# Staging the spatial weights earlier, and taking the high copies of normalized v from another source, in a fused attention and gated-MLP kernel

## The chip, the cores and the metric

The kernel runs as one program on one core of a Trainium2 chip. The metric is the time of one execution on the device in microseconds (us). Each version is timed in several runs, and one more execution is recorded by the hardware profiler. Every time below is of the kernel before the change.

## The reference

Three blocks follow each other on 4 batches of 576 tokens, 8 heads of 64, so 512 channels.

```python
# 1. attention, two masks: heads 0-3 local (the last 32 keys), heads 4-7 strided (every 32nd key)
scores = where(mask, q @ k.T / 8, -1e9)
attn   = exp(scores - max) / (sum + 1e-9)
x      = attn @ v                                    # [4, 576, 512]
# 2. gated block: v is normalized per token, then mixed over tokens
h = relu(x @ w_in);  u, v = h[..., :512], h[..., 512:]
v_n = (v - mean(v)) / sqrt(var(v) + 1e-6)            # over the 512 channels
v_s = einsum('ts,bsd->btd', w_spatial, v_n) + b_spatial
x   = (u * v_s) @ w_out
# 3. rotation block
theta = x @ w_theta
y = einsum(w_tok_r, x * cos(theta)) + einsum(w_tok_i, x * sin(theta))
u = x + y;  out = u + relu(u @ w_ch)
```

Inputs are float32. Square weights arrive as 64-bit words (float64 patterns viewed as integers), the spatial weights as float32.

## The kernel before

**Precision.** Large products run in float16 with a split: each operand is kept as a high part and a residual ("low"), and three passes (high by high, low by high, high by low) are added up in PSUM. So every operand costs a copy (high, mostly ScalarE) and a subtraction (low, VectorE or GpSimd) before it can be used.

**Tiling.** 576 tokens are four blocks of 128 and a tail of 64. Tiles of x, u and the rest lie transposed, channels on partitions; v lies with tokens on partitions, since it is normalized over channels. Blocks 0 and 1 of v make pair 0, blocks 2 and 3 pair 1. PSUM has three pairs of banks (tag "pm") that scores, v, u and all later products share, and two single banks ("sc", "av") for the attention of the following batches.

**The first attention** (`attention0`, line 658) has no other work to hide behind. It goes through nine groups of blocks in a pipeline of steps `s`: scores of group s, its exponentials, transposes of group s-1, the product with v of group s-2, and for group s-3 the transposed output, copied to `xT[0]` as high and low part (`gr_out`, line 617, ScalarE and then VectorE). Keys and queries of the two strided head pairs lie in the tile `xT[1]`, which is needed otherwise only when the attention of batch 1 writes its output there. Steps 9, 10 and 11 (`NG`, `NG+1`, `NG+2`) only drain the pipeline. In this phase every instruction keeps its place as written (`pinned`), on every engine and on the DMA-issuing queue SP.

Between the steps stand pieces of other work, given as a table (lines 1298 to 1309): the input weights `w_in` in four pieces of 1 MB, each with a load (`l0` to `l3`) and four conversion parts: two ScalarE passes in place on the 64-bit words (`a`, `b`), a VectorE combination (`c`), and the split (`e`: ScalarE high, GpSimd low). Pieces 0 and 1 are the v half, pieces 2 and 3 the u half. `go` emits the next stretch of the v product of batch 0; its last stretch reads channel block 3 of `xT[0]`, which the last groups of the attention write. `step` advances the attention of batch 1 (`attention1`, line 822): the first call loads, the second loads more and emits scores, softmax and division of its first step.

**After `pinned.clear()`** a planner orders the instructions of each engine by priorities and its own estimate of times. What is emitted when goes by a clock that counts the columns of the products emitted so far: `others()` (line 1272) takes a list `conv` of conversions with due times and the steps of the next attention. Instructions issued through `hv`, `ha`, `hg` stand 200 places ahead in priority.

**The spatial weights** (`sp_part`, line 306) are such conversions: two parts of 256 rows, loaded into the two raw staging buffers that the input weights used before (`stage()` alternates between `x2f` and `zf`), then a ScalarE copy with a scale and a VectorE residual into `wsp`. A tail of 64 rows and the bias follow (`sp_tail`).

**Normalizing v** (`norm`, `norm_q`, lines 1004 to 1027): statistics give mean and variance, `rstd` makes the reciprocal deviation by iterations on small tiles, VectorE normalizes each block in place in `vr`, ScalarE copies a pair to the high part of `vn`, VectorE subtracts for the low part. The spatial product of the first chunk reads both.

In the trace a load on SP waits, besides for its buffer, until the load eight places ahead of it in the queue has landed: the fourth piece for the third, the first load of spatial weights for the fourth piece.

Of the kernel before, what the change touches and what calls it, by code (L numbers as in the profile page):

```python
# [14 lines left out]
F32 = mybir.dt.float32  # L15
# [3 lines left out]
AF = mybir.ActivationFunctionType  # L19
ALU = mybir.AluOpType  # L20
# [25 lines left out]
E_VHI = 'aa'  # L46
# [12 lines left out]
CONV_SP = (20.0, 9.9, 1.9)  # L59
# [10 lines left out]
def kernel(  # L70
# [52 lines left out]
    nc = Engines  # L123
# [17 lines left out]
    B, DM, S = out.shape  # L141
    P = 128
    NC = DM // P
    NF = S // P
# [21 lines left out]
    hv, ha, hg = Ahead(nc.vector, AHEAD), Ahead(nc.scalar, AHEAD), Ahead(nc.gpsimd, AHEAD)  # L166
    H = {"v": hv, "a": ha, "g": hg}
    N = {"v": nc.vector, "a": nc.scalar, "g": nc.gpsimd}

    def copy(eng, key, dst, src):  # L170
        e = eng[key]
        if key == "a":
            e.activation(dst, src, AF.Copy)
        else:
            e.tensor_copy(dst, src)
# [30 lines left out]
    xT = [const.tile([P, 2, NC, S], F16, name=f"xT{i}") for i in range(2)]  # L206
    vn = const.tile([P, NF + 1, 2, DM], F16, name="vn")
# [9 lines left out]
    def s2(name):  # L217
        return scr.tile([P, 2, HS * 2], F32, tag="s2", name=name, bufs=4)
# [4 lines left out]
    def pm(name):  # L223
        return ps_m.tile([P, 2, 512], F32, tag="pm", name=name)
# [22 lines left out]
    def stage(late_raw=None):  # L247
        i = early[1]
        early[1] += 1
        if early[0]:  # L250
            return (raw0, raw1)[i % 2], vals[i % 2]
        return late_raw, s2("wx").rearrange("p a n -> p (a n)")
# [21 lines left out]
    def pair(ap, n):  # L274
        return ap[:, 0:2 * n].rearrange("p (a n) -> p a n", a=2)
# [12 lines left out]
    def prep_w(dst, src, c, i, late):  # L288
        for f in steps_w(dst, src, c, i, late):
            f()  # L290
# [11 lines left out]
    def sq_parts(dst, src, late=1):  # L302
        for i in range(0, NC, 2):
            yield lambda i=i: prep_w(dst, src, slice(0, DM), i, late)

    def sp_part(i):
        stg = pair(stage()[0].bitcast(F32), S)
        nc.sync.dma_start(stg, w_spT[i * P:(i + 2) * P, :].rearrange("(a p) n -> p a n", p=P))
        nc.scalar.activation(wsp[:, 0, i:i + 2, :], stg, AF.Copy, scale=SPS)
        nc.vector.scalar_tensor_tensor(wsp[:, 1, i:i + 2, :], stg, SPS, wsp[:, 0, i:i + 2, :],  # L310
                                       op0=ALU.mult, op1=ALU.subtract)
# [144 lines left out]
    NG = len(groups)  # L456
# [501 lines left out]
    def rstd(st, var, c):  # L958


        h, y, t = st[:, 0, c], st[:, 1, c], st[:, 2, c]
        hv.tensor_scalar(h, var, 1e-6, 0.5 / VNS ** 2, op0=ALU.add, op1=ALU.mult)
        hv.tensor_scalar(t.bitcast(I32), h.bitcast(I32), 1, None, op0=ALU.logical_shift_right)
        hv.tensor_scalar(y.bitcast(I32), t.bitcast(I32), -1, 0x5EF759DF - 2 ** 31, op0=ALU.mult, op1=ALU.add)
        for it in range(3):
            hv.tensor_tensor(t, y, y, ALU.mult)
            hv.tensor_tensor(t, t, h, ALU.mult)
            hv.scalar_tensor_tensor(y, t, 1.5, y, op0=ALU.subtract, op1=ALU.mult)

    def tail_mm(ps, x, w, cols):  # L970


        for n, (xe, we) in enumerate(PASS):
            for i in range(2):
                for h in range(2):
                    c = 2 * h + i
                    mm(ps[TL * h:TL * h + TL, :], x[:, xe, c, T0:S], w[:, we, c, cols],
                       start=(n == 0 and i == 0), stop=(n == 2 and i == 1))
                clock[0] -= DM

    def fold_tail(dst, tmp, ps):
        ha.activation(tmp, ps[TL:P, :], AF.Copy)
        hv.tensor_tensor(dst, ps[0:TL, :], tmp, ALU.add)

    def main_v(b):
        xh = xT[b % 2]
        vr = {}
        mv = mvs[:, b % 2]
        rs = att_p.tile([P, 3, 8], F32, tag="rs", name="rs")
        def v_relu(pr, ps):  # L990
            v = vr[pr] = s2(f"vr{pr}")
            if pr == 2:
                fold_tail(v[0:TL, 0, 0:DM], v[0:TL, 1, 0:DM], ps[:, 0, :])
                ha.activation(v[0:TL, 0, 0:DM], v[0:TL, 0, 0:DM], AF.Relu, scale=1.0 / PS)
                rows, nt = TL, 1
            else:
                ha.activation(v[:, :, 0:DM], ps, AF.Relu, scale=1.0 / PS)
                rows, nt = P, 2
            bs = att_p.tile([P, 2, 6], F32, tag="bs", name="bs")
            for t in range(nt):  # L1000
                hv.bn_stats(bs[0:rows, t, :], v[0:rows, t, 0:DM])
                hv.bn_aggr(mv[0:rows, 2 * pr + t, :], bs[0:rows, t, :])

        def norm(qs):
            c = slice(2 * qs[0], min(2 * qs[-1] + 2, 5))
            rstd(rs, mv[:, c, 1], c)
            for q in qs:
                norm_q(q)

        def norm_q(q):  # L1010
            rows = P if q < 2 else TL
            nt = 2 if q < 2 else 1
            for t in range(nt):
                i = 2 * q + t
                vv = vr[q][0:rows, t, 0:DM]
                hv.tensor_scalar(vv, vv, mv[0:rows, i, 0:1], rs[0:rows, 1, i:i + 1],
                                        op0=ALU.subtract, op1=ALU.mult)
            if q < 2:
                sv = vr[q][:, 0:2, 0:DM]
                copy(H, E_VHI[b > 0], vn[:, 2 * q:2 * q + 2, 0, :], sv)  # L1020
                H[E_VLO[q + 2 * (b > 0)]].tensor_tensor(vn[:, 2 * q:2 * q + 2, 1, :], sv,
                                                              vn[:, 2 * q:2 * q + 2, 0, :], ALU.subtract)
            else:
                sv = vr[2][0:TL, 0, 0:DM]
                copy(H, E_VHI[b > 0], vn[0:TL, 4, 0, :], sv)
                hv.tensor_tensor(vn[TL:P, 4, 0, :], sv, vn[0:TL, 4, 0, :], ALU.subtract)
                hg.tensor_copy(k2[0:TL], vn[0:TL, 4, 0, :])

        def v_mm(ps, i, c):
            for n, (xe, we) in enumerate(PASS):  # L1030
                clock[0] += DM
                marks.append((clock[0] / 2400.0, nc.tensor.matmul(
                    ps, xh[:, xe, c, i * P:(i + 1) * P], win[:, we, c, DM:2 * DM],
                    start=(c == 0 and n == 0), stop=(c == NC - 1 and n == 2)).ins.name))

        if b == 0:
            ps = [pm("v0")]

            def some(pr, cs, ts=(0, 1)):
                for t in ts:  # L1040
                    for c in cs:
                        v_mm(ps[pr][:, t, :], 2 * pr + t, c)

            for t in range(2):
                some(0, (0, 1), (t,))
                yield
            some(0, (2,))
            ps.append(pm("v1"))
            some(1, (0, 1))
            yield  # L1050
            some(1, (2,))
            yield
            for pr in range(2):
                some(pr, (3,))
                yield
                v_relu(pr, ps[pr])
            norm((0, 1))
        for pr in V_ORDER if b else V_ORDER[2:]:
            ps = pm(f"v{pr}")
            if pr == 2:  # L1060
                tail_mm(ps[:, 0, :], xh, win, slice(DM, 2 * DM))
                yield
            else:
                for t in range(2):
                    for c in range(NC):
                        v_mm(ps[:, t, :], 2 * pr + t, c)
                    yield
            v_relu(pr, ps)
        norm((2,) if b == 0 else (0, 1, 2))

    def main_mid(b):
# [164 lines left out]
    def timed(parts, due, lead, gap):  # L1236
        parts = list(parts)
        for i, f in enumerate(parts):
            conv.append((due - lead - gap * (len(parts) - 1 - i), f))

    timed([lambda i=i: sp_part(i) for i in range(0, NF, 2)] + [sp_tail], *CONV_SP)
    timed(sq_parts(wout, w_out), *CONV_OUT)
    timed(sq_parts(wth, w_th), *CONV_TH)
    conv.append((conv[-1][0], switch))
# [10 lines left out]
    for at, f in [(at, lambda n=n: tok_load(*toks[n])) for n, at in enumerate(TOK_AT)] + [  # L1255
            (at, lambda: next(atts[N32])) for at in PREP_AT]:
        i = next((i for i, c in enumerate(conv) if c[0] > at), len(conv))
# [32 lines left out]
    l1, a1, b1, c1, e1 = win_steps(1, 2)  # L1290
    l2, a2, b2, c2, e2 = win_steps(0, 0)
    l3, a3, b3, c3, e3 = win_steps(0, 2)
    v0 = main_v(0)

    def go():
# [6 lines left out]
        5: ((), (e0, l2)),  # L1302
        6: ((), (a1, b1)),
        7: ((), (c1, step)),
        8: ((), (e1, l3, go)),
        NG: ((), (go, step)),
        NG + 1: ((), (go, a2, b2, c2)),
        NG + 2: ((), (go, e2, a3, b3, c3, e3)),
    })
    pinned.clear()  # L1310
    run_main(v0)
# [93 lines left out]
```

## Time and profile before

| | us |
|---|---|
| median of 3 runs (lowest, highest) | 489.07 (488.37, 489.84) |
| profiled execution, whole | 488.06 |
| its span in the trace | 486.3 |
| TensorE matmul busy | 468.4 (96%) |
| VectorE busy | 300.8 (62%) |
| ScalarE busy | 267.2 (55%) |
| GpSimd busy | 71.4 (15%) |

Shares are means over stages with different limits: what a part of the program costs is read from the stage that it lies in. The granted clock of TensorE is 1.0 of full speed in all of the span. In the rows below, a timeline row gives the start, the length, the engine, the line (107 for all of them, since one helper issues every instruction), the operation, output and inputs, the tile's shape, how many were merged, and in brackets how long the engine had stood idle and what ended that.

### The profile page before, as it was taken

The numbers are of one execution on the slowest core, as the hardware profiler recorded it, in microseconds if no ns is written. First come the engines' busy times: TensorE is split into PE (matmuls) and PEld (weight loads), VectorE is DVE, ScalarE is ACT, GpSimd is POOL, SyncE is SP. The second block draws the span as 40 slices with busy tenths as digits, with TensorE's granted clock in tenths as the row PEclk, the third lists the DMA queues.
The fourth block names the chain that finished last, engine by engine and source line by source line (L and its number), as shares of the span: only waits on it lengthen the run. The fifth ranks groups of instructions, "written<-read, shape, count | busy, mean of one in ns | idle before, by whom it ended". The sixth has DMA issues, their size and how long they took to land. (4 is left out here: it accounts for less than half of the span.)

```text
span 486.3 us, 10776 instructions
## 1 busy us (share of the span) xinstructions
PE 468.4 (96%) x4440; PEld 352.3 (72%) x4440; DVE 300.8 (62%) x642; ACT 267.2 (55%) x470; POOL 71.4 (15%) x68
## 2 busy tenths in 40 slices
PE   7889889899999999999999999999999999999996
PEld 5665667676577778777568777777567777777775
DVE  3766998966998546752787878762686121227412
ACT  2657788879954334445945667754942022149202
POOL 2041124120015100201005100111005200210320
PEclk9999999999999999999999999999999999999999
DMA  6887666638760245100381345320450020003502
GB/s 179 288 243 208 201 224 217 195 154 245 161 148 1 69 163 148 54 0 1 86 217 52 91 123 158 67 44 1 74 122 1 2 98 0 1 2 76 121 0 99
DMA packets 71820, 52.72 MB, mean 108 GB/s; under 512 B 50584, under 2 KB 59992, under 8 KB 71770
## 3 DMA queue, kind: packets, MB, share of 16 engines
q1 hardware_dynamic: 71466, 51.42, 38.3%
q8 instruction: 35, 0.57, 0.5%
q10 hardware_dynamic: 304, 0.61, 0.4%
q14 instruction: 15, 0.12, 0.1%
HBM read 35.36 MB, written 4.72 MB: 82 GB/s over the span
## 5 line engine op out<-in xcount | busy, mean ns | idle before, releaser
L107 PE MATMUL y<-wtok,zf 128*128 128x288 f16 x864 | 107.2, 286 | 0.0
L107 PEld LDWEIGHTS <-zf 128*128 128x128 f16 x864 | 84.1, 98 | 22.2 <-issue 1.2
L107 PE MATMUL sp<-wsp,vn 128*128 128x288 f16 x384 | 50.3, 286 | 0.8 <-ACT u L107 0.8
L107 PE MATMUL x<-zf,wout 128*128 128x288 f16 x384 | 49.6, 287 | 0.0
L107 PE MATMUL u<-xT,win 128*128 128x288 f16 x384 | 49.3, 286 | 0.0
L107 PE MATMUL v<-win,xT 128*128 128x512 f16 (+1 forms) x240 | 48.4, 380 | 0.8 <-DVE xT L107 0.6
L107 PEld LDWEIGHTS <-vn 128*128 128x128 f16 x416 | 40.3, 98 | 11.2 <-issue 0.9
L107 PE MATMUL th<-x2h,wth 128*128 128x288 f16 x384 | 47.9, 286 | 0.3 <-DVE ta L107 0.3
L107 POOL TENSOR_TENSOR x2h<-x2f,x2h 128x576 f16<-128x576 f32 x19 | 26.6, 1403 | 142.7 <-issue 66.7
L107 PE MATMUL c<-x2h,wch 128*128 128x288 f16 x360 | 45.2, 286 | 0.0
L107 PEld LDWEIGHTS <-wth 128*128 128x128 f16 x384 | 37.6, 98 | 10.0 <-issue 0.5
L107 PEld LDWEIGHTS <-wch 128*128 128x128 f16 x384 | 37.4, 98 | 9.3
L107 PEld LDWEIGHTS <-win 128*128 128x128 f16 x384 | 37.4, 98 | 9.2
L107 PEld LDWEIGHTS <-wout 128*128 128x128 f16 x384 | 36.7, 98 | 9.5
L107 PEld LDWEIGHTS <-xT 128*128 128x128 f16 (+1 forms) x240 | 21.0, 100 | 25.3 <-issue 2.2
L107 ACT ACTIVATE x2h<-x2f 128x576 f16<-128x576 f32 (+1 forms) x28 | 20.9, 748 | 24.0 <-DVE x2f L107 23.5
L107 ACT ACTIVATE o<-c 128x576 f32<-128x576 f32 x15 | 9.7, 645 | 34.9 <-PE c L107 34.7
L107 DVE TENSOR_TENSOR ta<-ta,x2f 128x1152 f32<-128x1152 f32 (+1 forms) x17 | 21.7, 1284 | 11.2 <-ACT ta L107 11.2
L107 DVE SCALAR_TENSOR_TENSOR x2f<-y,x2f 128x576 f32<-128x576 f32 x16 | 12.1, 754 | 25.1 <-PE y L107 25.0
L107 DVE SCALAR_TENSOR_TENSOR o<-x2f,o 128x576 f32<-128x576 f32 (+1 forms) x17 | 12.2, 722 | 23.6 <-ACT o L107 23.6
L107 POOL TENSOR_TENSOR zf<-u,zf 128x576 f16<-128x576 f32 x8 | 10.2, 1277 | 112.9 <-ACT zf L107 112.9
L107 DVE TENSOR_TENSOR u<-u,sp 128x576 f32<-128x576 f32 x16 | 12.0, 750 | 22.4 <-PE sp L107 22.4
(146 smaller groups left out, 723.7 us busy)
## 6 DMA issues: line engine op xcount, KB each, us to landing
out_dram<-o SPq DMA_DIRECT2D x15, 288.0 KB
kt<-in_qp_dram SPq DMA_DIRECT2D x8, 288.0 KB
qs<-in_qd_dram SPq DMA_DIRECT2D x8, 288.0 KB
x2f<-in_w_in_dram SPq DMA_DIRECT2D x2, 1024.0 KB
zf<-in_w_in_dram SPq DMA_DIRECT2D x2, 1024.0 KB
xT<-in_w_ch_dram SPq DMA_DIRECT2D x2, 1024.0 KB
kt<-in_kzl_dram SPq DMA_DIRECT2D x8, 152.0 KB
ks<-in_kl_dram SPq DMA_DIRECT2D x4, 304.0 KB
```

What stands on the lines that cost most here:

```text
L107: ins = f(*args, **kwargs)
```

## The change

The two parts of the spatial weights no longer use the alternating staging buffers. They are loaded into `xT[1]` (`sp_place`, `sp_load`), issued behind the last load of input weights, and converted in step 11 of the first attention, no longer by the clock; only `sp_tail` stays in the timed list. In the table of the first attention the conversion of pieces 2 and 3 moves one step ahead (`a2`, `b2`, `c2` to step 9, `e2`, `a3`, `b3` to step 10), and the second `step` of batch 1 moves from step 9 to step 11, between the two conversions.

For batch 0, the high copies of the normalized v of the four full blocks are made by ScalarE from the unnormalized v with a per-partition scale (the reciprocal deviation) and bias (minus mean times that, one small VectorE product), one instruction for each block. VectorE's normalized v goes to other tiles (`vq` for pair 0, `vr[0]` for pair 1) and serves the residuals.

```diff
--- before.py
+++ after.py
@@ -303,9 +303,16 @@
         for i in range(0, NC, 2):
             yield lambda i=i: prep_w(dst, src, slice(0, DM), i, late)
 
+    raw_sp = xT[1].rearrange("p e c n -> p (e c n)").bitcast(F32)
+
+    def sp_place(i):
+        return raw_sp[:, i * S:(i + 2) * S].rearrange("p (a n) -> p a n", a=2)
+
+    def sp_load(i):
+        nc.sync.dma_start(sp_place(i), w_spT[i * P:(i + 2) * P, :].rearrange("(a p) n -> p a n", p=P))
+
     def sp_part(i):
-        stg = pair(stage()[0].bitcast(F32), S)
-        nc.sync.dma_start(stg, w_spT[i * P:(i + 2) * P, :].rearrange("(a p) n -> p a n", p=P))
+        stg = sp_place(i)
         nc.scalar.activation(wsp[:, 0, i:i + 2, :], stg, AF.Copy, scale=SPS)
         nc.vector.scalar_tensor_tensor(wsp[:, 1, i:i + 2, :], stg, SPS, wsp[:, 0, i:i + 2, :],
                                        op0=ALU.mult, op1=ALU.subtract)
@@ -1004,8 +1011,18 @@
         def norm(qs):
             c = slice(2 * qs[0], min(2 * qs[-1] + 2, 5))
             rstd(rs, mv[:, c, 1], c)
+            if b == 0 and qs[0] == 0:
+                hv.scalar_tensor_tensor(rs[:, 0, c], mv[:, c, 0], -1.0, rs[:, 1, c], op0=ALU.mult, op1=ALU.mult)
+                vr.update({3: s2("vq"), 4: vr[0]})
+                for i in range(4):
+                    ha.activation(vn[:, i, 0, :], vr[i // 2][:, i % 2, 0:DM], AF.Identity,
+                                  bias=rs[:, 0, i:i + 1], scale=rs[:, 1, i:i + 1])
             for q in qs:
                 norm_q(q)
+
+        def normed(q):
+
+            return q + 3 if b == 0 and q < 2 else q
 
         def norm_q(q):
             rows = P if q < 2 else TL
@@ -1013,11 +1030,12 @@
             for t in range(nt):
                 i = 2 * q + t
                 vv = vr[q][0:rows, t, 0:DM]
-                hv.tensor_scalar(vv, vv, mv[0:rows, i, 0:1], rs[0:rows, 1, i:i + 1],
+                hv.tensor_scalar(vr[normed(q)][0:rows, t, 0:DM], vv, mv[0:rows, i, 0:1], rs[0:rows, 1, i:i + 1],
                                         op0=ALU.subtract, op1=ALU.mult)
             if q < 2:
-                sv = vr[q][:, 0:2, 0:DM]
-                copy(H, E_VHI[b > 0], vn[:, 2 * q:2 * q + 2, 0, :], sv)
+                sv = vr[normed(q)][:, 0:2, 0:DM]
+                if b:
+                    copy(H, E_VHI[1], vn[:, 2 * q:2 * q + 2, 0, :], sv)
                 H[E_VLO[q + 2 * (b > 0)]].tensor_tensor(vn[:, 2 * q:2 * q + 2, 1, :], sv,
                                                               vn[:, 2 * q:2 * q + 2, 0, :], ALU.subtract)
             else:
@@ -1238,7 +1256,7 @@
         for i, f in enumerate(parts):
             conv.append((due - lead - gap * (len(parts) - 1 - i), f))
 
-    timed([lambda i=i: sp_part(i) for i in range(0, NF, 2)] + [sp_tail], *CONV_SP)
+    timed([sp_tail], *CONV_SP)
     timed(sq_parts(wout, w_out), *CONV_OUT)
     timed(sq_parts(wth, w_th), *CONV_TH)
     conv.append((conv[-1][0], switch))
@@ -1302,10 +1320,10 @@
         5: ((), (e0, l2)),
         6: ((), (a1, b1)),
         7: ((), (c1, step)),
-        8: ((), (e1, l3, go)),
-        NG: ((), (go, step)),
-        NG + 1: ((), (go, a2, b2, c2)),
-        NG + 2: ((), (go, e2, a3, b3, c3, e3)),
+        8: ((), (e1, l3, lambda: sp_load(0), lambda: sp_load(2), go)),
+        NG: ((), (go, a2, b2, c2)),
+        NG + 1: ((), (go, e2, a3, b3)),
+        NG + 2: ((), (go, c3, lambda: sp_part(0), e3, step, lambda: sp_part(2))),
     })
     pinned.clear()
     run_main(v0)
```

## Rows read from the trace of the kernel before

**Rows 1.** The page, busy us (share of the span) and instructions of each engine.

```profile
PE 468.4 (96%) x4440; PEld 352.3 (72%) x4440; DVE 300.8 (62%) x642; ACT 267.2 (55%) x470; POOL 71.4 (15%) x68
```

**Rows 2.** Stages: length, busy us of each engine, TensorE clock, DMA share, GB/s.

```profile
31.30:49.00 17.70, 17.38 (x156) 9.62 (x156) 10.51 (x26) 11.47 (x17) 6.41 (x7) 1.00 0.87 228
49.00:75.00 26.00, 22.85 (x236) 16.73 (x234) 25.88 (x70) 21.80 (x33) 7.33 (x7) 1.00 0.63 211
75.00:110.00 35.00, 32.05 (x419) 24.72 (x420) 28.16 (x49) 28.79 (x43) 7.56 (x6) 1.00 0.56 184
110.00:480.00 370.00, 367.96 (x3272) 279.56 (x3271) 214.87 (x442) 187.87 (x350) 44.67 (x31) 1.00 0.31 78
```

**Rows 3.** Timeline of TensorE.

```profile
36.01 0.73 PE L107 MATMUL a<-kt 64*64 64x96 f32 x16
...
37.95 4.06 PE L107 MATMUL v<-win,xT 128*128 128x512 f16 x18
...
42.07 5.46 PE L107 MATMUL v<-win,xT 128*128 128x512 f16 x30
...
58.49 0.61 PE L107 MATMUL av<-ident,sm 128*96 128x128 f32 x4 [1.52 <-ACT wspt L107]
...
62.34 1.63 PE L107 MATMUL sp<-wsp,vn 128*128 128x288 f16 x12 [0.76 <-ACT u L107]
```

**Rows 4.** Timeline of VectorE.

```profile
37.05 0.56 DVE L107 TENSOR_REDUCE st<-a 128x4 f32<-128x384 f32 x1 [1.27 <-PE a L107]
...
38.79 0.55 DVE L107 TENSOR_REDUCE st<-sm 128x4 f32<-128x384 f32 x1 [0.59 <-ACT sm L107]
...
42.65 0.38 DVE L107 TENSOR_TENSOR xT<-at,xT 128x216 f16<-128x216 f32 x1
...
45.81 1.35 DVE L107 SCALAR_TENSOR_TENSOR x2h<-zf,x2h 128x1024 int32<-128x1024 int32 x1 [2.78 <-DMA x2f<-in_w_spT_dram]
...
47.09 1.28 DVE L107 BATCH_NORM_STATS2 bs<-vr 128x6 f32<-128x512 f32 x2
...
50.63 1.48 DVE L107 SCALAR_TENSOR_TENSOR wsp<-x2f,wsp 128x1152 f16<-128x1152 f32 x1
...
52.77 1.34 DVE L107 SCALAR_TENSOR_TENSOR wsp<-zf,wsp 128x1152 f16<-128x1152 f32 x1
...
57.79 0.55 DVE L107 TENSOR_TENSOR sm<-sm,st 128x384 f32<-128x384 f32 x1
...
58.26 1.91 DVE L107 TENSOR_SCALAR vr<-vr,mv,rs 128x512 f32<-128x512 f32 x4
...
61.05 2.36 DVE L107 TENSOR_TENSOR vn<-vr,vn 128x1024 f16<-128x1024 f32 x2
```

**Rows 5.** Timeline of ScalarE.

```profile
34.53 0.38 ACT L107 ACTIVATE smx<-at 128x256 f32<-128x256 f32 x1
...
38.98 1.12 ACT L107 ACTIVATE x2f<-x2f 128x1024 f32<-128x1024 f32 x1
...
40.00 1.13 ACT L107 ACTIVATE x2h<-x2f 128x1024 int32<-128x1024 uint8 x1
...
42.27 0.35 ACT L107 ACTIVATE xT<-at 128x216 f16<-128x216 f32 x1 [1.13 <-PE at L107]
...
50.73 0.62 ACT L107 ACTIVATE vr<-vr 64x512 f32<-64x512 f32 x1
...
59.75 2.00 ACT L107 ACTIVATE vn<-vr 128x1024 f16<-128x1024 f32 x2
```

**Rows 6.** Timeline of the DMA-issuing queue SP.

```profile
33.76 0.39 SPq L107 DMA_DIRECT2D zf<-in_w_in_dram  x1
...
36.96 2.54 SPq L107 DMA_DIRECT2D v<-in_vl_dram  x4
...
42.66 0.38 SPq L107 DMA_DIRECT2D x2f<-in_w_spT_dram  x1
```

**Rows 7.** Waits of SP from 41 to 43 us: total, times, longest.

```profile
SPq L107 <- DMA zf<-in_w_in_dram: 1.7, 1, 1.7
```

## The prediction

> **What bounds the kernel now.** I read the busy shares first, then the stages side by side, then each engine's timeline in the stage that the diff touches, then what the DMA queue waits for.
>
> TensorE is busy for 468.4 of 486.3 us [rows 1]. The stages say where the rest lies: from 110 to 480 us it stands still for 2.0 us in all, and from 31.3 to 49 us for 0.3 us. From 49 to 75 us it loses 3.15 us and from 75 to 110 us 2.95 us; in the first of these two VectorE is busy for 25.88 of 26.00 us [rows 2]. The reader is to see two things there. The edit's ceiling is about 6 us, because little idle time lies behind it before the last outputs. And from 49 to 75 us VectorE is the engine that the others wait for, while from 31.3 to 49 us it has 7.2 us free (10.51 busy of 17.70).
>
> TensorE's waits are single instructions: 1.52 us ahead of the transposes of probabilities of batch 1, which start when VectorE's division ends (57.79 + 0.55 = 58.34), and 0.76 us ahead of the first spatial product [rows 3, 4]. The first wait is put down to ScalarE's tail of the spatial weights, which ended at about the same moment; the division makes the operand.
>
> **The change part by part.** The sum is made against the profiled execution: 488.06 us, of which 486.3 are the span and 1.8 lie around it. The median of the runs is 489.07, so 1.0 is added at the end.
>
> *Spatial weights.* Two ScalarE copies and two VectorE residuals (1.48 and 1.34 us) leave 49 to 54 us and go into the last steps of the first attention, whose order is fixed. Nothing is removed: 2.82 us of VectorE change places. That pays only if VectorE was idle there [rows 4].
>
> *Softmax of batch 1, first step.* It moves from behind step 9 to behind step 11. Its scores are TensorE's row at 36.01, some 0.9 us with the masks. VectorE's part is four operations of 0.55 to 0.56 and two small ones, which I put at 0.2 each since they touch 4 columns instead of 384: 2.6 in all, now begun at 37.05, and after the change behind 44 [rows 3, 4].
>
> *The order on ScalarE, worked out.* Its copy in step 9 ends at 34.53 + 0.38 = 34.91. The conversion of the third weight piece (a2, b2) now follows at once instead of at 38.98. The two passes take 40.00 + 1.13 - 38.98 = 2.15 us, so to 37.06 [rows 5]. VectorE's combination c2 (1.35, as c3 at 45.81) ends at about 38.4, the attention work behind it and ScalarE's e2 at about 39.5 [rows 4]. Next in the fixed order stands a3, which needs the fourth piece, and only behind a3 and b3 stands the copy of the last attention group into xT. Before, that copy stood ahead of them.
>
> When does the fourth piece land? It is issued at 33.76, behind the same loads as now. The queue's next loads are all issued at 36.96 + 2.54 = 39.50, and then the queue waits 1.7 us for that very piece [rows 6, 7]: about 41.2. What follows it in the queue changes (spatial weights instead of keys and values), what stands ahead of it doesn't. So a3 starts at 41.2, b3 ends at 43.35, the xT copy (0.35) at 43.7 and VectorE's residual (0.38) at 44.1. Before, the residual ended at 42.65 + 0.38 = 43.03 [rows 4, 5].
>
> *TensorE.* Without the scores it comes 0.9 us earlier through the v products. They run at 4.06/18 = 0.22 us, so the six of the third channel block, which begin at 42.07, end at 43.4 before and at 42.5 after [rows 3]. All that is left for it then needs the last group's xT: the v products of the fourth block read it, and the moved scores need a PSUM pair, of which there are three, two held by v and one by that group. TensorE waits from 42.5 to 44.1, **1.6 us**, where now it waits for nothing. It ends v at 49.0 instead of 47.5 (42.07 + 5.46).
>
> *VectorE.* Between 35.8 and 45.8 it now idles 1.27 + 0.59 + 2.78 = 4.64 us [rows 4]. After: 1.3 (to 37.06) and 4.2 (39.5 to 43.7), 5.5. It comes out 0.9 us behind, and up to 0.2 more for the added product of mean and reciprocal deviation: **1.0 us** later with the same work left. The idle time that the moved residuals were to fill lies ahead of the landing at 41.2.
>
> *High copies of normalized v.* Two ScalarE copies (2.00 together) become four of half the width. Bounds: half of 1.00 each, 2.0 in all, and 1.00 each, 4.0; I take the row with the same 512 columns, 0.62, so 2.5 [rows 5]. ScalarE is busy for 21.80 of 26.00 us there [rows 2], which covers the 0.5; without that cover they cost 0.5. The Trainium skill (ScalarE: Activation LUTs, What ACT_TABLE_LOAD costs) counts about 93 ns more for each per-partition operand, by which the four would be an estimated 2.8; no row shows a copy with both operands, and nothing else here goes by that. What changes is latency: today VectorE does four normalizations (1.91 from 58.26), ScalarE the copies (from 59.75), and from 61.05 VectorE the residuals (2.36) [rows 4, 5]. After, copies and normalizations start together, and the first residual can follow two normalizations, 61.05 - 58.26 - 0.96 = 1.8 us earlier. VectorE's total stays. So at most the wait of 0.76 ahead of the first spatial product goes, and at least nothing; I take 0.76.
>
> *New cost behind it.* The transposes of the moved softmax step wait for nothing now. After, VectorE ends its division behind c3, a weight residual, the step's own first half, one pair of statistics and the second half: 44.1 + 1.35 + 1.48 + 1.1 + 1.3 + 1.5 = 50.8 [rows 4], when TensorE is at about 49.8 with the next scores. The planner can put u products in between. So 0 to 1.0; I take 0.5.
>
> *Loads.* Later pieces of weights are loaded earlier, since their staging buffers come free. TensorE waits for none of them from 49 to 110 us, so I count zero, and up to 0.5 either way.
>
> **Sum.** +1.6 on TensorE at 44, +0.5 at the transposes, -0.8 at the first spatial product, and -0.8 at the wait of 1.52, because TensorE comes some 1.8 later to a VectorE that is 1.0 later: +0.5. From the other side: VectorE is full up to 75 us and 1.0 later, less what the shorter chain gives, so 0 to +1.0. The two agree. 488.06 + 0.5, and 1.0 for the median, is **489.5**.
>
> **Rivals.**
> - *No stall: the piece is there.* If a3 finds its data at 39.5, b3 ends at 41.7, xT is complete at 42.4 and TensorE never waits. VectorE's idle time is then 1.3 + 2.5 = 3.8, which after the added product is 0.7 less than now. The waits of 1.52 and 0.76 shrink to about 0.8 and 0, with up to 0.5 lost at the transposes: -1.0, and -2.5 if the planner fills all. That is 486.5 to 488.1, 487.2 in the middle. For it: the queue's wait may be put down to the wrong load, and the loads that share the DMA engines with the piece change. Against it: the queue's idle time from 39.50 to 42.66 has room for the named wait. The Trainium skill (DMA: Bandwidth & Descriptors, Anatomy of one DMA) fits 2.0 us plus the bytes at 436 GB/s, for the other kind of queue; an estimate by it for the piece of 1 MB is 4.4 us, a landing at 38.2, and this rival. The trace's 41.2 speaks against it: loads of keys and values stand ahead of the piece.
> - *Slower: the moved softmax step comes late, and what is in order behind it.* The place is the transposes at about 50 us; the price is 1.0 there and as much at the step after it. It decides if VectorE does the statistics and the second weight residual (1.34) ahead of the division and ends it past 51.5. With the 1.6, and 0.8 back at the spatial product, that is +1.6 to +2.8: 490.7 to 491.9. For it: the wait of 1.52 is of just this kind. Against it: the u products can go first.
> - *The new copies change nothing*, because VectorE takes all normalizations first, as now. That adds 0.8 to the forecast: 490.3, inside its own range.
>
> **How the numbers follow.** Forecast with its last variant 0.45, no stall 0.26, late softmax 0.29. A measurement of this kernel tells about 0.3%, 1.5 us, from no change. The forecast's own range is 488.0 to 490.6, nearly all of it within that bound. No stall falls mostly below it, late softmax above. So faster 0.25, same 0.45, slower 0.30. To hold 8 in 10 the range goes to 487.0 and 491.6.
>
> **What would show it.** In the profile after: ScalarE idle ahead of the fourth piece's first pass, ended by its load, near 41; the last xT residual near 44 instead of 43.0; TensorE with a wait of 1 to 2 us between 42 and 44.5, and v ending near 49; the four high copies beginning together with the normalizations; no wait at the first spatial product. The prediction is wrong if a3 starts before 40, if TensorE has no wait between 40 and 45, or if from 49 to 110 us it waits for less than 4 us or more than 8.

## The result: slower by 1.4%, and the profile after

The change made the kernel slower: 496.10 us (median of 6 runs, 495.49 to 498.63) against 488.75 (6 runs, 487.68 to 489.93), a ratio of 1.0137 with a 95% interval of 1.0117 to 1.0156. The prediction was 489.5, in a range up to 491.6. The profiled execution is the longest of the six: 498.63 us, of which 496.8 are the span. So its stretches below show about 3 us more loss than the 7.35 by which the medians differ.

The page after, busy us (share of the span) and instructions, then the granted clock of TensorE in 40 slices:

```profile
PE 472.9 (95%) x4440; PEld 355.2 (71%) x4440; DVE 303.4 (61%) x643; ACT 268.1 (54%) x472; POOL 73.0 (15%) x68
...
PEclk9899995999999999999999999999999999999999
```

TensorE has the same 4440 instructions as in [rows 1] and takes 4.5 us longer over them; in the slice from 74.5 to 86.9 us the clock is 5 tenths. Where the loss lies is seen with marks in the work as borders: the first scores of the last attention group, the first spatial product, and the first product with `w_out`. The stretches before (columns as in [rows 2]):

```profile
0.00:28.14 28.14, 22.93 (x296) 17.76 (x296) 16.66 (x48) 14.79 (x27) 3.38 (x17) 1.00 0.74 218
28.14:62.34 34.20, 31.09 (x321) 20.03 (x321) 26.85 (x77) 23.34 (x36) 10.31 (x9) 1.00 0.76 221
62.34:90.17 27.83, 25.61 (x350) 19.35 (x350) 25.90 (x48) 23.80 (x34) 10.23 (x9) 1.00 0.69 234
90.17:486.30 396.13, 388.73 (x3476) 295.15 (x3473) 231.40 (x472) 205.29 (x376) 47.43 (x33) 1.00 0.31 82
```

The same stretches after, then two that answer to [rows 2]:

```profile
0.00:29.89 29.89, 23.74 (x296) 18.61 (x296) 16.84 (x48) 14.73 (x27) 3.38 (x17) 0.94 0.72 201
29.89:63.68 33.79, 31.31 (x322) 19.98 (x321) 24.60 (x66) 24.19 (x36) 9.62 (x9) 1.00 0.84 256
63.68:102.06 38.38, 29.49 (x351) 21.38 (x351) 33.10 (x65) 26.23 (x37) 12.03 (x9) 0.87 0.51 164
102.06:496.80 394.74, 388.39 (x3476) 295.23 (x3473) 228.85 (x468) 202.98 (x375) 47.93 (x33) 1.00 0.31 80
...
49.00:75.00 26.00, 21.25 (x229) 15.58 (x224) 24.17 (x70) 20.26 (x31) 4.09 (x4) 1.00 0.54 185
75.00:110.00 35.00, 29.38 (x346) 21.59 (x347) 28.23 (x48) 22.57 (x33) 11.20 (x9) 0.85 0.57 185
```

The span is 10.5 longer: +1.75 in the first stretch, where the program is the same and the clock was 0.94 in this execution; -0.41 up to the first spatial product, which is the stretch that the prediction worked out; **+10.55** from there to the first product with `w_out`; and -1.39 behind it. So to compare a time of after with one of before up to 64 us, take 1.75 off. The 10.55 are 38.38 - 29.49 - (27.83 - 25.61) = 6.67 us more idle time and 3.88 us more busy time for practically the same instructions (351 and 350).

The stretch, in TensorE's timeline after:

```profile
45.05 0.61 PE L107 MATMUL v<-win,xT 128*128 128x512 f16 x2 [0.48 <-ACT xT L107]
...
53.85 0.61 PE L107 MATMUL av<-ident,sm 128*96 128x128 f32 x4 [0.29 <-DVE rs L107]
...
58.62 0.61 PE L107 MATMUL av<-ident,sm 128*96 128x128 f32 x4
...
63.68 1.88 PE L107 MATMUL sp<-wsp,vn 128*128 128x288 f16 x14 [0.75 <-ACT u L107]
...
70.86 0.45 PE L107 MATMUL sc<-pT,v 96*64 96x64 f32 x8
76.08 1.06 PE L107 MATMUL av<-ident,sm 128*96 128x128 f32 x4 [4.77 <-DVE sm L107]
78.94 0.69 PE L107 MATMUL sc<-pT,v 96*64 96x64 f32 x6 [1.79 <-ACT pT L107]
79.56 0.66 PE L107 MATMUL sp<-wspt,vn 128*128 128x288 f16 x2
...
81.78 4.82 PE L107 MATMUL sp<-wsp,vn 128*128 128x288 f16 x24
```

Two waits, 4.77 and 1.79, are nearly all of the added idle time. The row to look at is the one behind them, the tail part of the first spatial product (`sp<-wspt,vn`) at 79.56. In the kernel before it stood at 67.07, with 17 `u` products behind it and 20 spatial products from 72.31 on. A whole run of 24 took 3.10 us there (78.84):

```profile
67.07 0.42 PE L107 MATMUL sp<-wspt,vn 128*128 128x288 f16 x2 [0.17 <-DVE vn L107]
...
72.31 2.61 PE L107 MATMUL sp<-wsp,vn 128*128 128x288 f16 x20
...
78.84 3.10 PE L107 MATMUL sp<-wsp,vn 128*128 128x288 f16 x24
```

It needs the normalized tail of v (64 rows). ScalarE's rows for it, before, are its copy out of PSUM and, 16 us later, its high copy:

```profile
48.57 0.59 ACT L107 ACTIVATE vr<-v 64x512 f32<-64x512 f32 x1
...
64.92 0.62 ACT L107 ACTIVATE vn<-vr 64x512 f16<-64x512 f32 x1
```

ScalarE after:

```profile
42.59 1.15 ACT L107 ACTIVATE zf<-zf 128x1024 f32<-128x1024 f32 x1 [1.30 <-DMA zf<-in_w_in_dram]
...
44.66 0.33 ACT L107 ACTIVATE xT<-at 128x216 f16<-128x216 f32 x1
...
59.42 2.92 ACT L107 ACTIVATE vn<-vr,rs 128x512 f16<-128x512 f32 x4
62.36 0.59 ACT L107 ACTIVATE vr<-v 64x512 f32<-64x512 f32 x1
...
77.77 0.63 ACT L107 ACTIVATE vn<-vr 64x512 f16<-64x512 f32 x1 [2.47 <-DVE vr L107]
```

The tail is read out of PSUM at 62.36, behind the four new copies, where it used to be read at 48.57. From there on all that makes it is late. VectorE after:

```profile
45.02 0.38 DVE L107 TENSOR_TENSOR xT<-at,xT 128x216 f16<-128x216 f32 x1 [3.67 <-ACT xT L107]
...
62.37 1.23 DVE L107 TENSOR_TENSOR vn<-vq,vn 128x1024 f16<-128x1024 f32 x1 [1.43 <-ACT vn L107]
...
66.22 0.69 DVE L107 BATCH_NORM_STATS2 bs<-vr 64x6 f32<-64x512 f32 x1
...
69.83 1.11 DVE L107 TENSOR_TENSOR rs<-rs 128x1 f32<-128x1 f32 x1
...
74.39 1.55 DVE L107 TENSOR_TENSOR sm<-sm,st 128x384 f32<-128x384 f32 x1
75.86 1.11 DVE L107 TENSOR_TENSOR rs<-rs 128x1 f32<-128x1 f32 x1
...
78.44 0.69 DVE L107 TENSOR_TENSOR vn<-vr,vn 64x512 f16<-64x512 f32 x1 [0.70 <-ACT vn L107]
```

The tail's statistics come at 66.22, the iterations for its reciprocal deviation (`rs`, 128x1) lie scattered among softmax and conversions of `w_out` up to 77.2, and the residual ends at 79.1. The 4.77 is put down to a softmax division (74.39). That is only what stood first in TensorE's order; the experiments below ask whether the tail is the root.

### The profile page after: what moved, and what is told of

Its sections match the earlier page's. It is cut to its first block, busy times and chain, and to the rows that moved or that the text cites. A ratio compares the mean times of both kernels' runs of the same rounds, so it can differ in the third digit from the quotient of the medians.

```text
span 496.8 us, 10777 instructions
## 1 busy us (share of the span) xinstructions
PE 472.9 (95%) x4440; PEld 355.2 (71%) x4440; DVE 303.4 (61%) x643; ACT 268.1 (54%) x472; POOL 73.0 (15%) x68
## 5 line engine op out<-in xcount | busy, mean ns | idle before, releaser
L107 PE MATMUL sp<-wsp,vn 128*128 128x288 f16 x384 | 52.2, 292 | 0.8 <-ACT u L107 0.8
L107 PEld LDWEIGHTS <-vn 128*128 128x128 f16 x416 | 41.2, 100 | 11.7 <-issue 0.9
L107 POOL TENSOR_TENSOR x2h<-x2f,x2h 128x576 f16<-128x576 f32 x19 | 27.6, 1454 | 102.2 <-DVE x2h L107 46.0
L107 POOL TENSOR_TENSOR zf<-u,zf 128x576 f16<-128x576 f32 x8 | 11.2, 1405 | 118.0 <-ACT zf L107 113.6
```

The costliest lines, as they stand in the source:

```text
L107: ins = f(*args, **kwargs)
```

## The experiments

**Theory A, the tile.** The change takes one more tile for pair 0, `vq`, from the pool tag "s2" (four buffers), from which the tail takes its own, `vr2`. In the program text `vq`'s first write stands ahead of the tail's. If the planner gives `vq` its turn first, the tail can't be read out of PSUM before. **Rival B, the staging:** the moved softmax step and weight conversions cost the time. **Rival C, the copies:** four dependent ScalarE copies with two operands, and VectorE behind them, cost it.

All verdicts are ratios to the kernel before, run on the same chip (489.64 us beside e1, e2, e6 and e7; 489.23 beside e8 to e11; 489.34 beside e12 to e15). The stretch is that from the first spatial product to the first with `w_out`, in the one profiled execution. In that of e7 the clock fell behind a wait of 1.90 at 85.90 (0.94 over the stretch), so its stretch is longer than that of before, though its ratio is 1.0005.

| variant | median us | ratio (95%) | tail copied at | stretch |
|---|---|---|---|---|
| before | 488.75 | | 48.57 | 27.83 |
| the change | 496.10 | 1.0137 (1.0117 to 1.0156) | 62.36 | 38.38 |
| e1 staging only | 489.87 | 1.0005 (0.9970 to 1.0040) | 50.32 | 27.72 |
| e2 copies only | 496.10 | 1.0133 (1.0096 to 1.0171) | 60.70 | 34.13 |
| e6 tile only | 496.16 | 1.0130 (1.0081 to 1.0179) | 57.83 | 32.60 |
| e7 `vq` elsewhere | 490.13 | 1.0005 (0.9980 to 1.0031) | 49.21 | 30.41 |
| e11 tail first | 488.98 | 1.0003 (0.9983 to 1.0023) | 49.37 | 28.37 |

**e1: staging only**: the change without its edits of `norm`.

```diff
-                vr.update({3: s2("vq"), 4: vr[0]})
-                for i in range(4):
-                    ha.activation(vn[:, i, 0, :], vr[i // 2][:, i % 2, 0:DM], AF.Identity,
...
+                copy(H, E_VHI[b > 0], vn[:, 2 * q:2 * q + 2, 0, :], sv)
```

> Only the staging of the spatial weights and the new table of the first attention; normalization as before the change. Theory A (tile turn: vq, written only when the normalization begins, comes ahead of the tile of the v tail among the four s2 tiles, so the tail is read out of PSUM some 14 us late and its normalized rows reach the first spatial product 13 us late): no such wait, 488 to 491 us, tail copied before 53 us. Theory B (the moved softmax step and the fixed order on ScalarE make the transposes late by 4.8 us): 494 to 498 us, with the long TensorE wait near 71 us. Theory C (four ScalarE copies of 0.80 us instead of two of 1.0 us delay ScalarE): about 489 us.

The time is that of before, so B falls.

**e2: copies only**: the kernel before, with those edits of `norm` (e1's diff with the signs turned round).

> Only the normalization part (high copies by scale and bias, vq); staging and table as before the change. Theory A: the whole loss, 494 to 498 us, TensorE idle for over 4 us near 70 us and the granted clock at 0.5 behind it. Theory B: about 489 us. Theory C: 490 to 494 us without the late tail.

All the loss is there, and the tail is late (60.70). C had put it at 490 to 494 with the tail in time; but tile and copies stand in this run together, and e6 has to part them. One sign of A is met only in sum: TensorE waits 3.35 (73.71) and 1.45 (75.77), not over 4 in one. The clock is at 0.50 behind, from 76 to 80.

**e6: the tile alone.** The kernel before; pair 0 is normalized into a new tile, and the copies stay as they were.

```diff
+            if b == 0 and qs[0] == 0:
+                vr[3] = s2("vq")
...
-                hv.tensor_scalar(vv, vv, mv[0:rows, i, 0:1], rs[0:rows, 1, i:i + 1],
+                hv.tensor_scalar(vr[3 if b == 0 and q == 0 else q][0:rows, t, 0:DM], vv, mv[0:rows, i, 0:1], rs[0:rows, 1, i:i + 1],
...
```

> The kernel before with one thing changed: pair 0 of v is normalized into vq, a further s2 tile, instead of in place. ScalarE's copies as before, staging as before. Theory A: the loss is here alone, 493 to 498 us. Theories B and C: 488 to 490 us.

The loss is all there without a single new copy, so C falls as its cause. VectorE's first write of `vq`, ScalarE's row of the tail, and TensorE's of the tail product:

```profile
57.58 0.53 DVE L107 TENSOR_SCALAR vq<-vr,mv,rs 128x512 f32<-128x512 f32 x1
```

```profile
57.83 0.59 ACT L107 ACTIVATE vr<-v 64x512 f32<-64x512 f32 x1
```

```profile
74.12 0.42 PE L107 MATMUL sp<-wspt,vn 128*128 128x288 f16 x2 [1.94 <-DVE vn L107]
```

The tail's copy starts 0.25 behind the first write of `vq`.

**e7: the change, with `vq` elsewhere**, in a part of a large tile that is free at that time.

```diff
-                vr.update({3: s2("vq"), 4: vr[0]})
+                vq = zf[:, (NF + 1) * 2 * DM:(NF + 1) * 2 * DM + 4 * DM].bitcast(F32)
+                vr.update({3: vq.rearrange("p (a n) -> p a n", a=2), 4: vr[0]})
```

> The changed kernel, but vq lies in the part of zf that the gated tile fills later, so the v tail's s2 tile waits for nothing. Theory A: the loss goes, 487 to 491 us, tail copied before 54 us. Theory B: 494 to 498 us. Theory C: 490 to 494 us.

The loss is gone. The tail is copied at 49.21, and its product starts at 66.48. (The 490.13 lies inside C's range too; it is e6 that rules C out.)

**e11: the change, with the tail first.** The tile comes from the same pool of four; only the place of `norm((0, 1))` in the text differs.

```diff
-            norm((0, 1))
         for pr in V_ORDER if b else V_ORDER[2:]:
...
             v_relu(pr, ps)
+        if b == 0:
+            norm((0, 1))
         norm((2,) if b == 0 else (0, 1, 2))
```

> The changed kernel with vq again among the four s2 tiles, but the normalization of the full blocks is emitted behind the tail's relu, so the tail's tile has its turn first. If the turn is the cause (theory A1): tail copied before 54 us, no wait over 2 us near 71, 487 to 491 us. If four s2 tiles are too few for pair 0, pair 1, vq and tail at once (theory A2): the tail is late as in the changed kernel, or vq is, 493 to 498 us.

ScalarE and TensorE of e11:

```profile
49.37 0.59 ACT L107 ACTIVATE vr<-v 64x512 f32<-64x512 f32 x1
```

```profile
67.42 0.42 PE L107 MATMUL sp<-wspt,vn 128*128 128x288 f16 x2
```

The number of buffers is the same as in the change, and the loss is gone: what matters is the turn. (A fifth buffer of the tag was not tried.)

**e12: is it the transposes or the tail?** The change, with 22 more products of 128x512 into the bank of the transposes, ahead of those that waited 4.77. It was to keep TensorE busy, so that the clock's part could be read.

```diff
-                qd_turn(s - 1, sm, pa4("av"), pT)
+                pt = pa4("av")
+                if b == 1 and s == 4:
+                    for _ in range(22):
+                        nc.tensor.matmul(pt.rearrange("p n k -> p (n k)"), win[:, 0, 0, 0:P], win[:, 0, 0, DM:2 * DM],
+                                         start=True, stop=True)
+                qd_turn(s - 1, sm, pt, pT)
```

> The changed kernel with 22 extra v-sized products (0.216 us each, 4.7 in all) into the bank of the fourth transposes of batch 1; their result is overwritten. TensorE works through 20 of them where it stood idle from 71.3 to 76.1; the transposes come behind the first spatial product's tail. If the halved clock that follows the long wait is a part of the loss of its own (theory K): the granted clock stays at 1.0 and the time falls by 3 to 5 us, to 491 to 493. If the loss is only the waiting for the late tail of normalized v: clock or not, 494.5 to 497. In both, TensorE goes on with the first spatial product only when the tail's rows are there, at 77 to 79 us.

It took 498.77, ratio 1.0176 (1.0127 to 1.0225), above both ranges; why it is above them is open. TensorE of e12:

```profile
69.24 4.49 PE L107 MATMUL av<-win 128*128 128x512 f16 x20
77.17 0.42 PE L107 MATMUL sp<-wspt,vn 128*128 128x288 f16 x2 [3.44 <-DVE vn L107]
```

The planner put the transposes behind the tail product, and now the wait is for the tail itself: its normalized rows hold the spatial products back, not the division, which ended at 73.93. For the clock the run settles nothing: 3.44 us of idle time were left, and the clock fell again (0.91 over the stretch).

The other six asked what is left of the prediction's terms when the tail is not late.

**e9: no wait for the fourth piece.** e7, with `a3` and `b3` moved from step 10 to step 11, behind the last copy into `xT`.

```diff
-        NG + 1: ((), (go, e2, a3, b3)),
-        NG + 2: ((), (go, c3, lambda: sp_part(0), e3, step, lambda: sp_part(2))),
+        NG + 1: ((), (go, e2)),
+        NG + 2: ((), (go, a3, b3, c3, lambda: sp_part(0), e3, step, lambda: sp_part(2))),
```

> The changed kernel with vq in zf, and the first passes of the fourth weight piece behind the copy of the last attention group into xT instead of ahead of it. The prediction's step: that copy no longer waits for the landing, TensorE's wait ahead of the last v products (0.44 us with vq in zf) goes, and the time falls by 0.4 to 1.6 us against vq in zf alone: 488 to 489.7. Rival: VectorE is full behind it and the wait comes back there: the same 490 us.

489.98 us, ratio 1.0017 (0.9995 to 1.0040). TensorE has no wait there from 41.91 to 48.15, but it waits 0.48 for VectorE at 49.39, and 1.70 at the first spatial product (1.11 in e7). The time is that of e7 within what can be measured: as the rival had it, the wait came back further on.

**e10: the softmax step back in step 9**, with the table of before and the spatial parts in step 11, on e7.

```diff
...
+        NG: ((), (go, step)),
+        NG + 1: ((), (go, a2, b2, c2)),
+        NG + 2: ((), (go, e2, a3, b3, c3, lambda: sp_part(0), e3, lambda: sp_part(2))),
```

> The changed kernel with vq in zf, and the table as before the change but for the two spatial parts, which stand in step 11: the softmax step of batch 1 is back behind step 9. The prediction's term for the moved step: TensorE's wait at the transposes near 52 us (0.36) goes, VectorE has 2.6 us less behind 44 us, so 487.5 to 489 us. Rival: the place of the step is indifferent: 490 us.

492.67 us, ratio 1.0089 (1.0059 to 1.0120), above both forecasts. It doesn't tell about the step, since it made a new wait. TensorE, then GpSimd:

```profile
53.85 0.91 PE L107 MATMUL u<-xT,win 128*128 128x288 f16 x6 [2.31 <-POOL win L107]
```

```profile
51.14 3.77 POOL L107 TENSOR_TENSOR win<-x2h,win 128x512 f16<-128x512 f32 x2 [4.22 <-ACT win L107]
```

The last split of `w_in` came late for `u`. `e3` stands behind a spatial part in e7 too; here its piece is converted later as well, so that ScalarE comes to its half of `e3` at 50.02 (44.65 in e7) and GpSimd to the split at 51.14 (45.79), and the split took 3.77 (2.27).

**e8: copies only, `vq` elsewhere**: e2 with e7's diff.

> Only the normalization part, vq in the part of zf that the gated tile fills later; staging and table as before the change. The prediction's term for the copies: the wait ahead of the first spatial product (0.76 us) goes, 488 to 489 us (0 to 0.8 below the kernel before). Rival: four copies of 0.80 us cost ScalarE 1.2 us and VectorE waits for them, so the wait stays, 489 to 490.5 us.

491.61, ratio 1.0057 (1.0032 to 1.0081). That is above both forecasts, and the wait at the first spatial product didn't go (0.75).

**e14 and e15: the emission alone.** e14 is e2 with e11's diff; e15 is the kernel before with e11's diff and nothing else.

> Only the normalization part, emitted behind the tail's relu, with staging and table as before the change. If the 2.4 us of the same part with vq in zf came from the four copies themselves (1.2 us more of ScalarE): 490.5 to 492. If they came from the order that the planner found: 488.5 to 490, as with the new staging.

> The kernel before with its normalization emitted behind the tail's relu and nothing else: what the place of emission is worth by itself. If it is neutral: 488.5 to 490. If emitting later makes the first spatial product wait longer: 490 to 492.

e14 took 491.16, ratio 1.0030 (1.0005 to 1.0055), and e15 491.77, 1.0050 (1.0024 to 1.0075). Where `norm` stands in the text costs as much on the old staging without any new copy, so the price of the copies on the old staging can't be told from that of the planner's order. For e11, e15 says that the later place gains nothing by itself.

**e13: e11 and e9 together**, and `e3` ahead of the first spatial part.

```diff
...
+        NG + 1: ((), (go, e2)),
+        NG + 2: ((), (go, a3, b3, c3, e3, lambda: sp_part(0), step, lambda: sp_part(2))),
```

> The changed kernel with the normalization emitted behind the tail's relu, the first passes of the fourth weight piece behind the xT copy, and the u half's last split ahead of the first spatial part. The wait ahead of the last v products (0.26 us) goes; the waits at transposes stay: 488 to 489.5 us, from 0.8 below the kernel before to equal. Rival: as with vq in zf, the reordered table costs 0.5 to 1: 489.5 to 490.5.

493.24, ratio 1.0071 (1.0040 to 1.0102): 0.7% above the ratio of e11 and above both forecasts, with new waits of 1.14 at 49.88 and 1.24 at 73.47. e11 and e9 cost nothing that can be measured singly; whether their sum costs this or the moved `e3`, the run doesn't tell.

No variant is measurably faster than the kernel before; the nine without the late tail have ratios from 1.0003 to 1.0089.

## Why the prediction was wrong, step by step

**The step that failed** is "High copies of normalized v": "VectorE's total stays. So at most the wait of 0.76 ahead of the first spatial product goes, and at least nothing". It gave the copies and normalizations a price and the new tile none; neither the sum nor a rival has the pool's turn in it. The term was -0.76 with bounds of -0.76 and 0; the tile alone measured +6.5 (496.16 against 489.64). The two signs were there to see: the diff has `vr.update({3: s2("vq"), 4: vr[0]})`, of the same tag as the tail's `vr2`, and in the trace of before the tail's copy (48.57) stands 9.7 us ahead of the normalizations (58.26, [rows 4]). An allocation that stands in the text ahead of the tail's but is used after it turns that round.

The size follows from the order. The tail product moved from 67.07 to 79.56, 10.7 late after the shift. The work that could have filled the time, 24 spatial products (81.78), stands behind it in TensorE's order, and the `u` products were done before 70.9. So TensorE waited, 6.67 us more than before, and then took 3.88 longer over the same work. In 2-us slices (columns as in [rows 2]):

```profile
72.00:74.00 2.00, 0.00 (x0) 0.00 (x0) 2.00 (x8) 0.91 (x2) 0.04 (x1) 1.00 1.03 409
74.00:76.00 2.00, 0.00 (x0) 0.00 (x0) 2.00 (x7) 1.30 (x2) 1.64 (x2) 0.76 0.93 354
...
80.00:82.00 2.00, 2.00 (x22) 1.22 (x21) 1.26 (x2) 1.52 (x2) 0.00 (x0) 0.50 0.03 8
82.00:84.00 2.00, 2.00 (x10) 1.28 (x9) 2.00 (x4) 1.47 (x3) 0.20 (x1) 0.50 0.64 191
84.00:86.00 2.00, 2.00 (x13) 1.40 (x12) 0.78 (x2) 2.00 (x3) 2.00 (x2) 0.68 0.86 188
86.00:88.00 2.00, 2.00 (x51) 1.55 (x49) 0.88 (x3) 0.39 (x3) 0.08 (x1) 1.00 1.01 416
```

TensorE stands still from 71.3, the clock falls within 74 to 76, and from 80 to 86 TensorE is busy throughout at 0.50, 0.50 and 0.68: 24 spatial products take 4.82 us (81.78); before, 24 took 3.10 (78.84). That the clock turned a wait into a longer one is read from these rows; no run isolated it. Its part varies: the profile of e6 has less of it (stretch at 0.95, 32.60 us).

**The loads and ScalarE's order: right.** `a3` waits 1.30 for the fourth piece and starts at 42.59, which is 40.8 after the shift; predicted 41.2. The rival by which the piece is there earlier falls: it was issued at 34.81, so it was usable 7.8 us later, behind other loads. By the Trainium skill (DMA: Bandwidth & Descriptors, Anatomy of one DMA), whose fit is for the other kind of queue, an estimate was 4.4 us; the trace of this queue doesn't agree, and it decides. The last xT residual ends at 45.02 + 0.38, or 43.65 after the shift; predicted 44.1.

**TensorE's wait of 1.6 at 44: mis-sized.** It measured 0.48 (1.04 in e1, 0.26 in e11). The first products of the fourth block need only ScalarE's high copy (44.66), not VectorE's residual, and TensorE came there a little later than I worked out. e9 takes the wait away and gains nothing that can be measured.

**The moved softmax step: right in kind, and cheap.** Its transposes wait 0.29 (0.36 in e7); I took 0.5. The wait of 1.52 [rows 3] is gone (58.62); the sum took 0.8 of it. Nothing is gained by it even without the tile: e1 has waits of 1.04 at 44.24 and 0.35 at 53.72 in its place, and 1.25 instead of 0.76 at the first spatial product. The rival that the step comes late falls: e1 is at 1.0005.

**The wait of 0.76 at the first spatial product: wrong.** It stays, 0.75 (1.11 in e7, 1.61 in e11), put down to ScalarE's `u`. The four copies take 2.92, not 2.5. They come one behind the other, and VectorE waits 1.43 for them (62.37). So "copies change nothing" was the better variant. The estimate of 2.8 by the Trainium skill (ScalarE: Activation LUTs, What ACT_TABLE_LOAD costs) is near the 2.92. With the charge for two operands alone it would be 4 times 0.62 + 0.19, or 3.2; it comes to 2.8 by the overlap of instructions that follow one another, which the same section gives and the prediction didn't name.

**The sum without the tile.** With the tail in its turn (e11) the ratio is 1.0003, -0.25 us by the medians, and the forecast for it was +0.5: right within what can be measured, but in part by luck, since the terms at 44 (0.26 for 1.6) and at the first spatial product (1.61 where the sum had none) are off, and cancel.

**The signs.** `a3` doesn't start before 40, and there is a wait between 40 and 45 (0.48, over at 45.05). v ends at 50.10, or 48.35 after the shift; I named 49. From 49 to 110 us TensorE waits 4.75 + 5.62 = 10.4 us, more than the 8 that I named. Of the three signs of being wrong, that one alone told.

## What to carry to other kernels

Where a planner orders the instructions, a new tile is an instruction with a place in a queue: look up which tag it comes from, which tile takes the next turn, and when that tile is first written. Compare that time with the new tile's first write in the trace; if it is earlier, the later tile can inherit the difference, as here. And when a wait is put down to an engine, look behind the waiting instruction for what else stands there, since filling or moving the first one only shows the next (e12).

## What the runs showed of the hardware

TensorE's clock didn't come back with the work: after 4.77 us of idle time and some short products it stayed at 0.50 (1.2 of 2.4 GHz) while TensorE was busy without a break from 80 to beyond 84.

Small VectorE instructions became long beside GpSimd's subtractions for `w_out`. GpSimd after:

```profile
69.57 2.47 POOL L107 TENSOR_TENSOR wout<-x2h,wout 128x512 f16<-128x512 f32 x2 [19.59 <-ACT wout L107]
...
74.36 2.59 POOL L107 TENSOR_TENSOR wout<-x2h,wout 128x512 f16<-128x512 f32 x2 [2.32 <-ACT wout L107]
```

In these two stretches a product of 128x1 took 1.11 us (69.83 and 75.86; 0.14 for the one at 73.65) and a division of 128x384 1.55 (74.39; 0.55 in [rows 4]). e6 has the same: two products of 128x1 took 1.09 and 1.08 (67.81 and 68.93) inside GpSimd's 67.72 to 70.00. Not every instruction is longer there: the subtraction at 70.87, which reads the scores `a` from PSUM, took 0.55. VectorE after:

```profile
70.87 0.55 DVE L107 TENSOR_TENSOR sm<-a,st 128x384 f32<-128x384 f32 x1
...
73.65 0.14 DVE L107 TENSOR_TENSOR rs<-rs 128x1 f32<-128x1 f32 x1
```

That GpSimd is the cause is read from the times that fall together; no run takes its work away. A chain of small instructions, as the reciprocal deviation is, can pay this on several of its links.
